# Second layer's rows fetched by quarters, turned by VectorE instead of TensorE, with four output tiles

## The chip, the core and the metric

One core of a Trainium2 chip runs the whole program. The metric is device time in microseconds (us) for one execution; 0.5% of it is about 5 us. The engines are TensorE (PE: matmuls; PEld: its weight loads), VectorE (DVE), ScalarE (ACT), GpSimd (POOL) and SyncE (SP, which here only issues DMAs). Line numbers (L708) are those of the kernel before.

## What is computed

Three steps, each feeding the next (cut to what matters):

```python
x = attention(q, k, v, M_prev, z_prev, beta)        # 4 x 576 tokens, 8 heads of 64 -> 2304 x 512
# layer 1: one expert of 8 for each token
e = argmax(x @ w_gate + modality_bias[modality_id]); x = gate * relu(x @ w1[e]) @ w2[e]
# layer 2: two experts of 8 for each token, chosen with noise
logits = x @ w_gate2 + log1p(exp(x @ w_noise)) * noise
for e in range(8):
    for k in range(2):
        mask = top2[:, k] == e
        out[mask] += top2_w[mask, k, None] * (np.maximum(x[mask] @ w1[e], 0) @ w2[e])
```

Widths are D = 512 for a token and F = 1024 for the hidden layer; everything is float32.

## The kernel before, in words

**Precision.** Each float32 operand is split into a rounded high part and a remainder (`xh`/`xl`, `w1h`/`w1l`, `w2h`/`w2l`, `hh`/`hl`), and each product is three matmuls: high by high, remainder by high, high by remainder (L718 to L720 for `mm1`, L728 to L730 for `mm2`).

**Stages.** Attention runs first; its order on the engines is worked out at build time by a list scheduler (`Tasks`) from costs, priorities and dependencies. The DMAs that fill `out` and part of the DRAM table `xd` with zeros are SP tasks in that plan (L1109 to L1116). Layer 1 then walks over units of 256 tokens of one expert (`full`), or over two half units (`pair`). Each unit gathers its rows, computes them and writes the new tokens `x1` to `xd` (`x1_out`, L882). Beside the matmuls a generator `route2` computes the second layer's routing in small steps; what it finds is added to the table `M2` (L952), which says which slot of which expert holds which token.

**Layer 2** (`layer2`, from L976). Expert 0 is begun on the 256 slots that the last layer 1 unit left (224 used columns). Then `route2` ends, `slot_tables` makes the gather and scatter indices, three 128 row tiles of expert 0 are gathered and the rest of expert 0 runs. After that experts 1 to 7 run in turn, each on 640 slots, that is five tiles of 128. An expert has two stages on TensorE:

- `mm1`: eight blocks `f` of the hidden layer, each as two halves of 304 columns (expert 0: one piece of 384), 12 matmuls each. ACT makes `hh`, DVE makes `hl`, and both split `w2`.
- `mm2`: five tiles (expert 0: three) of 24 matmuls of 512 columns. ACT scales the tile into one of two `os` buffers (L972), and POOL scatters it to `out` with an adding indirect DMA (L973), in which each waits for the landing of the one before.

While `mm2` of expert e runs, expert e+1 is prepared. Five gathers (L701, 128 rows of 520 floats each) were issued on POOL at the start of expert e. A list `todo` is worked off between half tiles. It has eight splits of `w1` (`split_w1`) and five `xsplit`s: four TensorE transposes of 128x128 into PSUM (L708), an ACT copy to `xh` (L709) and a DVE subtraction to `xl` (L710). The transposes stand in TensorE's in-order stream between the matmuls of `mm2`. The weights of expert e+1 are loaded by SP when their buffers are free.

## Time and profile before

| | us |
|---|---|
| runs shown | 986.49, 987.15, 991.69 |
| their median | 987.15 |
| the profiled execution | 984.86 |
| its span on the chip (first to last instruction) | 983.1 |

| engine | busy us | share of the span |
|---|---|---|
| PE (matmul) | 943.0 | 96% |
| DVE | 555.5 | 56% |
| ACT | 488.2 | 50% |
| POOL | 353.2 | 36% |

Attention lasts to about 260 us, layer 1 to about 508, the first 256 slots of layer 2 and its tables to about 540, the experts to about 969; the last scatters and the end of the program follow. A busy share is an average over stages with different limits, so the stages are read one by one. A row of the timeline has start, duration, engine, line, operation, output<-input, and in brackets the idle time before it with what ended that.

### The profile page before, as it was taken

The numbers are of one execution on the slowest core, as the hardware profiler recorded it, in microseconds if no ns is written. First come the engines' busy times: TensorE is split into PE (matmuls) and PEld (weight loads), VectorE is DVE, ScalarE is ACT, GpSimd is POOL, SyncE is SP. The second block draws the span as 40 slices with busy tenths as digits, with TensorE's granted clock in tenths as the row PEclk, the third lists the DMA queues.
The fourth block names the chain that finished last, engine by engine and source line by source line (L and its number), as shares of the span: only waits on it lengthen the run. The fifth ranks groups of instructions, "written<-read, shape, count | busy, mean of one in ns | idle before, by whom it ended". The sixth has DMA issues, their size and how long they took to land. (4 is left out here: it accounts for less than half of the span.)

```text
span 983.1 us, 18583 instructions
## 1 busy us (share of the span) xinstructions
PE 943.0 (96%) x6849; PEld 831.0 (85%) x6849; DVE 555.5 (56%) x1695; ACT 488.2 (50%) x1141; POOL 353.2 (36%) x420
## 2 busy tenths in 40 slices
PE   7999999999989999999997999999999999999994
PEld 5888888888875889888886999898989989898983
DVE  8777777789745577777775244243442424244320
ACT  6887878775433455555552244333342433343320
POOL 5222232244643567777765231121313021231111
PEclk9999999999989899999999999999999999999997
DMA  8345856262567555666655254536446354535112
GB/s 211 100 112 183 270 184 205 93 223 84 167 214 265 162 193 206 216 215 215 205 178 158 66 137 124 127 82 160 105 107 172 97 121 128 138 77 117 23 23 35
DMA packets 83840, 144.98 MB, mean 147 GB/s; under 512 B 14480, under 2 KB 32912, under 8 KB 83728
## 3 DMA queue, kind: packets, MB, share of 16 engines
q1 hardware_dynamic: 73168, 117.10, 36.4%
q0 software_dynamic: 10560, 26.47, 13.6%
q8 instruction: 60, 0.98, 0.4%
q14 instruction: 52, 0.43, 0.1%
HBM read 111.65 MB, written 31.97 MB: 146 GB/s over the span
## 5 line engine op out<-in xcount | busy, mean ns | idle before, releaser
L718 PE MATMUL b<-xh,w1h 128*128 128x304 f32 (+3 forms) x800 | 240.0, 300 | 3.1 <-ACT xh L709 1.3
L719 PE MATMUL b<-xl,w1h 128*128 128x304 f32 (+3 forms) x800 | 238.2, 298 | 3.8 <-DVEq L788 3.5
L720 PE MATMUL b<-xh,w1l 128*128 128x304 f32 (+3 forms) x800 | 237.1, 296 | 0.0
L723 DVE SCALAR_TENSOR_TENSOR hl<-b,hh 128x304 fp32r<-128x304 f32 (+3 forms) x200 | 90.7, 454 | 207.1 <-ACT hh L721 205.4
L728 PE MATMUL b<-w2h,hh 128*128 128x512 f32 x464 | 188.7, 407 | 0.0
L730 PE MATMUL b<-w2h,hl 128*128 128x512 f32 x464 | 182.2, 393 | 0.0
L973 POOL DMA_INDIRECT out_dram<-os,l2s x40 | 62.8, 1571 | 331.5 <-ACT os L972 253.3
L729 PE MATMUL b<-w2l,hh 128*128 128x512 f32 x464 | 181.6, 391 | 0.0
L721 ACT ACTIVATE hh<-b 128x304 fp32r<-128x304 f32 (+3 forms) x200 | 81.8, 409 | 172.7 <-PE b L720 172.6
L718 PEld LDWEIGHTS b<-xh,w1h 128*128 128x128 f32 x800 | 152.7, 191 | 9.3 <-DVE hl L723 4.1
L719 PEld LDWEIGHTS b<-xl,w1h 128*128 128x128 f32 x800 | 152.7, 191 | 4.8 <-DVEq L788 3.7
L720 PEld LDWEIGHTS b<-xh,w1l 128*128 128x128 f32 x800 | 152.9, 191 | 0.0
L730 PEld LDWEIGHTS b<-w2h,hl 128*128 128x128 f32 x464 | 87.5, 189 | 19.5
L729 PEld LDWEIGHTS b<-w2l,hh 128*128 128x128 f32 x464 | 88.0, 190 | 15.5
L728 PEld LDWEIGHTS b<-w2h,hh 128*128 128x128 f32 x464 | 87.7, 189 | 15.4
L151 ACT ACTIVATE p<-sm,l 128x128 f32<-128x128 f32 (+4 forms) x144 | 84.1, 592 | 16.9 <-DVE l L147 16.9
L698 DVE TENSOR_TENSOR w1l<-w1r,w1h 128x512 fp32r<-128x512 f32 x84 | 71.3, 857 | 22.0 <-ACT w1h L697 21.8
L710 DVE TENSOR_TENSOR xl<-b,xh 128x512 fp32r<-128x512 f32 x56 | 38.6, 689 | 73.9 <-ACT xh L709 73.7
L693 ACT CAST w2h<-w2r 128x512 fp32r<-128x512 f32 x128 | 78.5, 613 | 0.0
L709 ACT CAST xh<-b 128x512 fp32r<-128x512 f32 x56 | 32.9, 587 | 87.7 <-PE b L708 87.7
L697 ACT CAST w1h<-w1r 128x512 fp32r<-128x512 f32 x128 | 74.7, 620 | 0.3 <-DMA w1r<-in_w_dram 0.3
L972 ACT ACTIVATE os<-b,l2w 128x512 f32<-128x512 f32 x40 | 27.7, 691 | 94.1 <-PE b L730 47.6
(460 smaller groups left out, 1511.4 us busy)
## 6 DMA issues: line engine op xcount, KB each, us to landing
w1r<-in_w_dram SPq DMA_DIRECT2D x18, 2048.0 KB, 9.6
w2r<-in_w_dram SPq DMA_DIRECT2D x18, 2048.0 KB, 9.2
xd<-gs SPq DMA_DIRECT2D x24, 260.0 KB, 3.7
xd<-x SPq DMA_DIRECT2D x10, 520.0 KB, 10.3
out_dram<-gs SPq DMA_DIRECT2D x19, 256.0 KB, 4.0
k<-in_k_dram SPq DMA_DIRECT2D x16, 256.0 KB, 4.3
q<-in_q_dram SPq DMA_DIRECT2D x16, 256.0 KB, 3.5
v<-in_v_dram SPq DMA_DIRECT2D x16, 256.0 KB, 4.4
```

The source lines that it names most:

```text
L151: s.nc.scalar.activation(s.P[b,i,u][:,lh*n:lh*n+n],s.SM[b,i,u][:,lh*n:lh*n+n],AF.Exp,scale=-1.0,bias=L[:,0,c:c+1],accum_out=L[:,1,c:c+1])
L693: nc.scalar.copy(hi[c],raw[:,c])
L697: nc.scalar.copy(s.w1h[:,:,fs],s.w1r[:,:,fs])
L698: eng.tensor_sub(s.w1l[:,:,fs],s.w1r[:,:,fs],s.w1h[:,:,fs].bitcast(FT))
L718: nc.tensor.matmul(h[:,:n],s.w1h[:,k,fs],s.xh[:,k,cs],start=k==0,stop=False)
L719: nc.tensor.matmul(h[:,:n],s.w1h[:,k,fs],s.xl[:,k,cs],start=False,stop=False)
L720: nc.tensor.matmul(h[:,:n],s.w1l[:,k,fs],s.xh[:,k,cs],start=False,stop=k==KD-1)
L721: def mm1_a(s, h, f, c0, n): s.nc.scalar.activation(s.hh[:,f,c0:c0+n],h[:,:n],AF.Relu)
L723: cs=slice(c0,c0+n); s.nc.vector.scalar_tensor_tensor(s.hl[:,f,cs],h[:,:n],0.0,s.hh[:,f,cs].bitcast(FT),op0=OP.max,op1=OP.subtract)
L728: nc.tensor.matmul(y,s.hh[:,f,cs],s.w2h[f],start=f==0,stop=False)
L729: nc.tensor.matmul(y,s.hh[:,f,cs],s.w2l[f],start=False,stop=False)
L730: nc.tensor.matmul(y,s.hl[:,f,cs],s.w2h[f],start=False,stop=f==KF-1)
```

## The change

**Layout.** `x1_out` writes each pair of tiles twice: to `xd` as before and to a second DRAM table `xq` in which a token is four rows of 128 floats. The zero fill does the same for the slots that need it (24 more DMAs; the groups in the plan become seven instead of five).

**Gathers.** A tile of 128 tokens is fetched by four indirect DMAs of 128 quarter rows (512 bytes each) instead of one of 128 whole rows. DMA i puts quarter g of token 32i+t on partition 32g+t, in columns 128i to 128i+127. The indices `gq4` come from `quarter_tables`: `M2` is copied, four small matmuls with a selection matrix `sel4` (made by `quarter_sel` on POOL) spread it over the partitions, and two DVE operations finish it. Groups of four are spread over the expert: one at its start, two behind `hl` of blocks 3 and 6, two in `mm2` behind `w1l` (expert 0: 2, 4, 6 and one in `mm2`); a one column copy to `pace` on POOL makes each wait.

**Transposes.** `bsplit` turns the tile by one VectorE instruction that transposes blocks of 32x32, into one of two SBUF buffers `xt_`; ACT's copy and DVE's subtraction read that instead of PSUM. Partition p then holds features 4p to 4p+3, so layer 2's `w1` is loaded in that order (`by='(p c)'`). Expert 0's first three gathered tiles still go the old way.

**Output tiles.** `os` has four buffers instead of two; the two new ones lie where `ol2` and part of `yt` lay.

```diff
+        s.xq=s.dram.tile([4*SLOTS,D//4],FT,name='xq')
...
-        ...; s.os=cut(K0,8192,512,'os',2)
+        ...; s.os=cut(K0,8192,512,'os',2)+[T(OL,0,512,'os2'),T(K1,8704,512,'os3')]
...
+    def bsplit(s, g, c0):
+        nc=s.nc; x=s.xt_[s.xn%2]; s.xn+=1
+        nc.vector.transpose(x.rearrange('p j (s t) -> p s j t',s=4),g.rearrange('p (s d j) -> p s j d',s=4,j=KD))
+        nc.scalar.copy(s.xh[:,:,c0:c0+128],x)
+        nc.vector.tensor_sub(s.xl[:,:,c0:c0+128],x,s.xh[:,:,c0:c0+128].bitcast(FT))
...
-        s.nc.sync.dma_start(d[:,c:c+n] if isinstance(c,int) else d[:,bass.ds(c,n)],s.x1[:,:n])
+        ...; dq=s.xq[:].rearrange('(c p q) d -> p c (q d)',p=128,q=4)
+        for d,w in ((d,XW),(dq,D)): s.nc.sync.dma_start(d[:,c:c+n] if isinstance(c,int) else d[:,bass.ds(c,n)],s.x1[:,:n,:w])
...
+    def quarter_sel(s):
+        G=s.nc.gpsimd; f=s.sel4f
+        G.memset(f,0.0)
+        G.affine_select(f.rearrange('p s (g t) -> p s g t',g=4),f.rearrange('p s (g t) -> p s g t',g=4),pattern=[[-32,4],[0,4],[-1,32]],compare_op=OP.not_equal,fill=1.0,base=0,channel_multiplier=1)
+        G.tensor_copy(s.sel4,f)
+        for g in range(4): G.memset(s.qn[32*g:32*g+32],float(g))
+    def quarter_tables(s):
+        ...
+        V.tensor_copy(m,s.M2[:,0])
+        p=s.ps.tile([128,512],FT,name='sm')
+        for i in range(4): nc.tensor.matmul(p[:,i*NC2:(i+1)*NC2],s.sel4[:,i],m,start=True,stop=True)
+        V.tensor_scalar(f,p[:,:4*NC2].rearrange('p (s c) -> p s c',s=4),float(S0),0.0,op0=OP.add,op1=OP.max)
+        V.tensor_scalar(s.gq4,f,4.0,s.qn[:,0:1],op0=OP.mult,op1=OP.add)
+    def quarter_gather(s, c, t, behind=None):
+        if behind is not None: s.nc.gpsimd.tensor_copy(s.pace,behind.bitcast(FT))
+        for i in range(4):
+            s.nc.gpsimd.indirect_dma_start(out=s.gq[t][:,i*128:(i+1)*128],out_offset=None,in_=s.xq[:],in_offset=bass.IndirectOffsetOnAxis(ap=s.gq4[:,i,c+t:c+t+1],axis=0))
...
+            if f==5: s.quarter_sel()
             s.split_w(s.w2r,s.w2h,s.w2l,f,nc.vector if f<3 else nc.gpsimd)
...
             s.l2_out(wk,y,tb,t,out)
+        s.quarter_tables()
         for t in range(NE+2,T2): s.xsplit(ps,ge[t-NE],t*128)
...
-                g=s.l2_gather(wk,tb,(e+1)*TS)
+                s.quarter_gather((e+1)*TS,0)
...
+                at=(2,4,6) if not e else (3,6)
+                if nxt and f in at: s.quarter_gather((e+1)*TS,1+at.index(f),s.hl[:,f,C2-1:C2])
...
-            for t in range(T2): todo.insert(2*t+1,lambda t=t:s.xsplit(ps,g[t],t*128))
+            for t in range(T2): todo.insert(2*t+2 if t<4 else len(todo),lambda t=t:s.bsplit(s.gq[t],t*128))
+            later=[(0,4)] if not e else [(0,3),(2,4)]
...
+                        i=2*(t-ts[0])+q
+                        if later and i==later[0][0]: s.quarter_gather((e+1)*TS,later.pop(0)[1],s.w1l[:,0,(i+1)*128:(i+1)*128+1])
...
+            dma.append(lambda r=r: nc.sync.dma_start(M.xq[4 * (r - N):4 * (r - N) + 512].rearrange('(p q) d -> p (q d)', q=4), zt[:, :D]))
-        M.later = [Q.add(100 * (5 + j // 5), SP, 1000, f, [A.sunk[4 + j // 5]]) for j, f in enumerate(dma)]
+        M.later = [Q.add(100 * (5 + j // 7), SP, 1000, f, [A.sunk[4 + j // 7]]) for j, f in enumerate(dma)]
```

## Rows read from the trace of the kernel before

**Rows 1.** Busy time by stretch: attention, layer 1, layer 2's experts; columns in the first line.
```profile
core 0: us, PE busy (x) PEld busy (x) DVE busy (x) ACT busy (x) POOL busy (x), PEclk, DMA share, GB/s
0.00:260.00 260.00, 249.48 (x2604) 213.14 (x2605) 202.95 (x820) 195.25 (x543) 85.08 (x112) 0.99 0.55 172
322.00:508.00 186.00, 185.12 (x1266) 164.59 (x1266) 142.58 (x433) 105.30 (x224) 130.96 (x173) 0.99 0.60 200
562.00:915.00 353.00, 353.00 (x2068) 319.45 (x2067) 138.27 (x234) 134.18 (x266) 80.06 (x62) 1.00 0.48 119
```

**Rows 2.** Groups of PE instructions by line, 545 to 903 us: the transposes.
```profile
L708 PE MATMUL b<-ident,gs 128*128 128x128 f32 x140 | 20.8, 272 | 0.0
```

**Rows 3.** Timeline of PE in expert 6: one block of transposes.
```profile
888.02 0.39 PE L730 MATMUL b<-w2h,hl 128*128 128x512 f32 x1
888.25 0.60 PE L708 MATMUL b<-ident,gs 128*128 128x128 f32 x4
888.61 0.48 PE L728 MATMUL b<-w2h,hh 128*128 128x512 f32 x1
888.92 0.40 PE L729 MATMUL b<-w2l,hh 128*128 128x512 f32 x1
```

**Rows 4.** Busy time by stretch: mm1 of expert 6, mm2 of experts 6 and 7.
```profile
858.84:885.50 26.66, 26.66 (x193) 26.66 (x192) 12.45 (x23) 11.10 (x24) 8.29 (x7) 1.00 0.35 73
885.50:915.17 29.67, 29.67 (x143) 24.51 (x141) 9.31 (x15) 10.02 (x18) 6.29 (x4) 1.00 0.51 107
941.84:969.06 27.22, 27.22 (x122) 22.35 (x120) 0.67 (x2) 3.18 (x5) 6.20 (x4) 1.00 0.30 37
```

**Rows 5.** Timelines of PE and DVE where the rest of expert 0 begins.
```profile
537.23 1.04 PE L708 MATMUL b<-ident,gs 128*128 128x128 f32 x8
538.49 0.69 DVE L710 TENSOR_TENSOR xl<-b,xh 128x512 fp32r<-128x512 f32 x1 [1.13 <-ACT xh L709]
539.55 0.69 DVE L710 TENSOR_TENSOR xl<-b,xh 128x512 fp32r<-128x512 f32 x1 [0.37 <-ACT xh L709]
539.57 0.45 PE L718 MATMUL b<-xh,w1h 128*128 128x384 f32 x1 [1.30 <-ACT xh L709]
```

**Rows 6.** Busy time by stretch, just behind that: the granted clock is PEclk.
```profile
541.30:544.70 3.40, 3.40 (x12) 3.40 (x12) 0.56 (x1) 0.49 (x1) 2.79 (x3) 0.52 0.95 164
545.00:547.00 2.00, 2.00 (x13) 2.00 (x12) 0.30 (x1) 0.49 (x1) 1.65 (x2) 1.00 0.74 216
```

**Rows 7.** Timelines of POOL, DVE and PE before the tables, and two POOL groups by line.
```profile
524.03 1.28 POOL L694 TENSOR_TENSOR w2l<-w2r,w2h 128x512 fp32r<-128x512 f32 x1 [1.50 <-ACT w2h L693]
524.05 1.29 DVE L941 SCALAR_TENSOR_TENSOR b<-ri,sv 128x4 f32<-128x4 int32 x1
525.26 0.72 POOL L938 CAST wh<-w__8256 128x4 fp32r<-128x4 f32 x1
527.82 0.74 PE L949 MATMUL b<-rrm,ol 128*128 128x256 f32 x4 [0.67 <-DVE rrm L946]
...
L1100 POOL MEMSET gs<- 128x520 f32 x1 | 0.5, 539 | 0.0
L123 POOL TENSOR_SCALAR ph<-q 128x512 f32<-128x512 f32 x4 | 5.9, 1491 | 9.1 <-PE b L175 8.9 <-DVE l L147 0.2
```

**Rows 8.** Gathers: timeline of POOL, landing of layer 2's, and the slowest form.
```profile
541.19 1.02 POOL L701 DMA_INDIRECT gs<-xd,l2g  x1 [0.30 <-issue]
542.51 0.98 POOL L701 DMA_INDIRECT gs<-xd,l2g  x1 [0.30 <-issue]
...
DMA to landing us min/median/max: 3.6/3.9/5.8
...
L701 POOL DMA_INDIRECT gs<-xd,nxi x10: 1250/1388/1499, 381.7 to 488.2; - x10
```

**Rows 9.** One line's instructions on DVE, ns min/median/max, whole span.
```profile
L694 DVE TENSOR_TENSOR w2l<-w2r,w2h x83: 684/693/715, 252.0 to 941.3; 128x512 fp32r<-128x512 f32 x83
```

More of the change, by code (lines that the diff above doesn't have):

```diff
@@ L357, in blocks @@
         K0,K1,X,HL,W2,G,X1,OL=range(8)
-        s.w1r=V(T(K0,0,4096,'w1r'),KD); s.w2r=V(T(K0,4096,4096,'w2r'),KF); s.os=cut(K0,8192,512,'os',2)
+        s.w1r=V(T(K0,0,4096,'w1r'),KD); s.w2r=V(T(K0,4096,4096,'w2r'),KF); s.os=cut(K0,8192,512,'os',2)+[T(OL,0,512,'os2'),T(K1,8704,512,'os3')]
         s.w1h=V(T(K1,0,4096,'w1h',FR),KD); s.w1l=V(T(K1,4096,4096,'w1l',FR),KD); s.yt=V(T(K1,8192,1024,'yt'),KD); s.rr=c.tile([128,4,256],FR,name='rrm')
@@ L365, in blocks @@
         s.wb1=V(T(W2,0,4096,'wb1'),KD); s.wb2=V(T(W2,4096,4096,'wb2'),KF)
+        s.gq=cut(G,0,D,'gq',GB); s.xt_=[V(t,KD) for t in cut(X1,0,D,'xtq',2)]; s.xn=0; s.sel4=V(T(K1,8192,512,'sel4',FR),4); s.sel4f=V(T(K1,8704,512,'sel4f'),4)
         s.x1=V(T(X1,0,2*XW,'x1'),2); s.ol2=V(T(OL,0,512,'ol2',FR),4); s.gs=cut(G,0,XW,'gs',GB); s.gn_=s.on_=0
@@ L686, in tasks, with load_w @@
         Q.add(P+14,POOL,300,lambda:nc.gpsimd.memset(s.rr[:,:,4*NC2:].bitcast(FT),0.0))
-    def load_w(s, raw, w, e, eng=None):
-        src=(w[bass.ds(e,1)] if not isinstance(e,int) else w[e:e+1]).rearrange('o (c p) f -> p (o c) f',p=128)
+    def load_w(s, raw, w, e, eng=None, by='(c p)'):
+        src=(w[bass.ds(e,1)] if not isinstance(e,int) else w[e:e+1]).rearrange('o %s f -> p (o c) f'%by,p=128)
         (eng or s.nc.sync).dma_start(raw,src)
@@ L703, in o, with xsplit @@
     def o(s):
-        s.on_+=1; return s.os[s.on_%2]
-    def xsplit(s, ps, g, c0):
+        s.on_+=1; return s.os[s.on_%len(s.os)]
+    def bsplit(s, g, c0):
[3 more added lines that the diff above has]
+        nc.vector.tensor_sub(s.xl[:,:,c0:c0+128],x,s.xh[:,:,c0:c0+128].bitcast(FT))
+    def xsplit(s, ps, g, c0, fourth=False):
         nc=s.nc
         tp=ps.tile([128,KD,128],FT,name='tp')
-        for k in range(KD): nc.tensor.transpose(tp[:,k],g[:,k*128:(k+1)*128],s.ident)
+        for k in range(KD): nc.tensor.transpose(tp[:,k],g[:,k:D:4] if fourth else g[:,k*128:(k+1)*128],s.ident)
         nc.scalar.copy(s.xh[:,:,c0:c0+128],tp)
@@ L736, in state @@
         nc=s.nc; c=s.c
+        s.qn=c.tile([128,1],FT,name='qn'); s.pace=c.tile([128,1],FT,name='pace')
         s.run=c.tile([128,E],FT,name='run'); nc.gpsimd.memset(s.run,float(DEAD))
@@ L880, in x1_out @@
     def x1_out(s, c, n):
-        d=s.xd[N:].rearrange('(c p) d -> p c d',p=128)
-        s.nc.sync.dma_start(d[:,c:c+n] if isinstance(c,int) else d[:,bass.ds(c,n)],s.x1[:,:n])
+        d=s.xd[N:].rearrange('(c p) d -> p c d',p=128); dq=s.xq[:].rearrange('(c p q) d -> p c (q d)',p=128,q=4)
+        for d,w in ((d,XW),(dq,D)): s.nc.sync.dma_start(d[:,c:c+n] if isinstance(c,int) else d[:,bass.ds(c,n)],s.x1[:,:n,:w])
     def route2(s, wk, ps, u, nt):
@@ L973, in l2_out @@
         nc.gpsimd.indirect_dma_start(out=out,out_offset=bass.IndirectOffsetOnAxis(ap=si[:,c:c+1],axis=0),in_=o,in_offset=None,compute_op=OP.add)
+    def quarter_sel(s):
[5 more added lines that the diff above has]
+    def quarter_tables(s):
+        nc=s.nc; V=nc.vector; m=s.c.tile([128,NC2],FR,name='mq'); f=s.c.tile([128,4,NC2],FT,name='fq'); s.gq4=s.c.tile([128,4,NC2],I32,name='gq4')
+        V.tensor_copy(m,s.M2[:,0])
[7 more added lines that the diff above has]
+            s.nc.gpsimd.indirect_dma_start(out=s.gq[t][:,i*128:(i+1)*128],out_offset=None,in_=s.xq[:],in_offset=bass.IndirectOffsetOnAxis(ap=s.gq4[:,i,c+t:c+t+1],axis=0))
     def l2_gather(s, wk, tb, c, ts=range(T2)):
@@ L983, in layer2 @@
         s.finish(); s.x1_out(s.nf*2+(FC-4),2)
-        s.load_w(s.w1r,w1,E+1)
+        s.load_w(s.w1r,w1,E+1,by='(p c)')
         s.chain=s.route2(wk,ps,NF+NP2,2); s.hold=0
@@ L1013, in layer2 @@
             if nxt:
-                if e: s.load_w(s.w1r,w1,E+e+1)
-                g=s.l2_gather(wk,tb,(e+1)*TS)
+                if e: s.load_w(s.w1r,w1,E+e+1,by='(p c)')
+                s.quarter_gather((e+1)*TS,0)
             for f in range(KF):
@@ L1077, in overflow @@
                 e=nc.values_load(ov[0:1,o:o+1],engines=[ET.SP],min_val=0,max_val=E-1)
-                s.load_w(s.w1r,w1,e+E); s.load_w(s.w2r,w2,e+E)
+                s.load_w(s.w1r,w1,e+E,by='(p c)'); s.load_w(s.w2r,w2,e+E)
                 for ff in range(KF): s.split_w1(ff,nc.vector)
-                for t,g in enumerate(s.l2_gather(wk,tb,o*T2)): s.xsplit(ps,g,t*128)
+                for t,g in enumerate(s.l2_gather(wk,tb,o*T2)): s.xsplit(ps,g,t*128,True)
                 for ff in range(KF):
```

## The prediction

> **What bounds the kernel now.** I read the busy times by stretch first [rows 1]. From 562 to 915 us, where experts 1 to 7 run, PE is busy for 353.00 of 353.00 us at a granted clock of 1.00, while DVE has 138, ACT 134 and POOL 80. Nobody keeps PE waiting there: whatever leaves PE's in-order stream in this stretch shortens the run by its whole length, and work given to DVE, ACT or POOL is free as long as its result comes in time. In attention PE is busy for 249 of 260 us and in layer 1 for 185 of 186, so those stages are bound by PE as well, and the change takes nothing from PE there. Next I read the groups by line for what leaves (140 transposes of L708 between 545 and 903 us [rows 2]), then PE's timeline around one block for its price [rows 3], and last the place where the new tables are made [rows 5 to 7].
>
> **The change part by part.**
>
> *Transposes leave PE.* An `xsplit` is four transposes, so 140 of them are 35 blocks, five in each of seven experts. In [rows 3] a matmul of 512 columns starts 0.23 us after the one before (888.02 to 888.25). From the first transpose to the second matmul behind the block it is 0.67 us (888.25 to 888.92), of which 0.23 is that first matmul's own, so a block costs 0.44 us. 35 x 0.44 = 15.4 us. A second reading bounds it: `mm2` of expert 6 takes 29.67 us with five blocks and of expert 7 without any 27.22 us [rows 4]. The 2.45 us of difference hold 2.2 us of blocks and 0.25 us of matmuls that run slightly slower beside the splits of ACT and DVE; 7 x 2.45 = 17.2 us is the upper end. I take 15.4, since ACT and DVE still do the splits.
>
> *What takes their place.* DVE gets one block transpose of 128x512 per tile. The trace has none; DVE operations of that size take 0.69 us [rows 9]. In `mm2` DVE is busy for 9.31 of 29.67 us [rows 4], so five transposes are hidden up to (27.2 - 9.3) / 5 = 3.6 us each. ACT's copy and DVE's subtraction stay, with the other source. Cost 0.
>
> *Gathers.* Each expert has 20 gathers of 64 KB instead of 5 of 260 KB. On POOL one gather starts 1.3 us after the other (541.19, 542.51) and layer 2's land 3.9 us after issue, 5.8 at most [rows 8]. A group of four then takes 5.3 us, five groups 26 us of an expert of about 54, with five scatters beside them. I follow the latest group for experts 1 to 6, from the start of the expert. Block 6 has its `hl` at 7/8 of 26.66 us [rows 4] and about 1.3 us more, 24.6. Three groups follow, with a scatter and its wait between them (about 1.9): POOL is done at 42.4, the rows are there at 46.3 and split (transpose, copy, subtraction) at 48.3. They are wanted by the second half of the next expert's first block, at 26.66 + 27.22 + 1.67 (26.66 / 16) = 55.5. So 7 us are to spare. Queued on POOL behind the `pace` waits are only further gathers and the scatters; the scatters come up to 4 us later, for which the four `os` buffers are there. Cost 0.
>
> In expert 0 it is tight. Its `mm1` has 96 matmuls of 384 columns (26.66 / 192 x 384 / 304 = 0.175 us each), 16.8 us, and its three tiles 3 x 5.44 = 16.3 us, so the last rows are wanted after 16.8 + 16.3 + 1.7 = 34.8 us. The group behind block 2 can start at about 7.3 us, and four groups in a row end at 28.5; landing (3.9) and split (2.0) give 34.4. I count 0, but see the first rival.
>
> *The tables.* `quarter_tables` stands in PE's stream between the second and third block of transposes at the start of expert 0, and its matmuls wait for a DVE copy that is queued behind the second tile's subtraction. Before, both blocks go as one run at 537.23, that subtraction ends at 539.18, and `mm1` begins at 539.57, when the third tile's ACT copy is done [rows 5]. Now: 539.18, the copy of 48 columns 0.2, four small matmuls 0.5, the third block 0.44, the ACT copy and its hand-overs 0.75, so `mm1` begins at about 541.1, and its second matmul moves with the third subtraction by as much. Everything behind moves too: +1.6 us (1.0 to 2.5).
>
> *The clock there.* [...] I take 0.
>
> *The selection matrix.* `quarter_sel` puts three POOL operations on 512 columns and four short ones ahead of the `w2l` split of block 5. [Rows 7] bound the long ones by 0.54 us (a memset of 520) and 1.49 us (one input, 512 columns); with the short ones 2.0 to 4.9 us. I take 2.6, nearer to the memset, since none of them calculates. POOL has 1.50 us of idle time before its last split, so `wh` (525.26), which `route2` ends on and for which DVE and then PE's L949 wait (0.67), comes about 1.1 us later. The first gathers come later by as much, but they wait today behind a weight load that does not move, so part of it is absorbed. +0.8 us (0 to 2.5). DVE can suffer beside POOL: an operation on four columns that starts with a POOL split lasts 1.29 us, as long as the split [rows 7]. [...] The rows speak against it for gathers: two-input splits of 128x512 last 0.715 us at most, though some run beside gathers [rows 9].
>
> *DMAs.* The second `x1_out` DMA (0.5 MB) stands on SP ahead of a weight load in each layer 1 unit, and the zero fill has 24 more in attention. The mean DMA share is 0.60 and 0.55 [rows 1], and PE is at 185 of 186 us, so loads come early enough now. The plan of attention sees more SP tasks ahead of its loads, which are issued several chunks early. +0.3 us (-1.5 to +2). The other order of `w1` moves the same 2 MB, in longer runs: 0. The two more `os` buffers shorten no wait of PE; at the end each scatter waits for the one before, not for a buffer: 0.
>
> *Sum.* -15.4 + 1.6 + 0 + 0.8 + 0.3 = -12.7 us. The profiled execution took 984.86 us (span 983.1), so the same execution would take 972.2. It lies 2.3 us below the median of the runs, 987.15; taken off that, 974.5 us.
>
> **The rivals.**
>
> 1. *Expert 0's last group is late.* It has 0.4 us to spare. In layer 1 the gathers by `nxi` take 1.39 us on POOL instead of 0.95 to 1.02 [rows 8]. If quarter gathers are of that kind, the pitch is 1.7, the 16 gathers in a row end 6 us later, and PE stands still for 5.5 us and gets the lower clock again (1.6): 974.5 + 7 = 981.5 us. For it: no row shows a gather of 512 byte rows. Against: the same form of index, and smaller pieces to land.
>
> 2. *POOL becomes the bound, and the kernel slower than before.* With pitch p, experts 1 to 6 need 24.6 + 12p + 7.8 us and have 55.5, so it decides from p = 1.93; expert 0 loses 16 (p - 1.3) - 0.4. At p = 2.2 that is 6 x 12 x 0.27 + 14 = 33 us: about 1008 us. It undoes the gain from p = 2.0 up. Against: the slowest gather, 1.50 us with 0.30 between, makes 1.8 [rows 8]. [...]
>
> 3. *DVE becomes the bound, no change.* At 4.1 us per transpose DVE needs all that PE gave back in `mm2`, and the time is about 986 us. Its read steps over four floats, which no row shows; but six times the price of any DVE operation of this size would be needed.
>
> **How the numbers follow.** About 0.5% (5 us) is what a measurement of this kernel can tell from no change. The forecast has a chance of 0.73. With all its terms at their good ends it gives 984.86 - 17.2 + 1.0 - 1.6 - 1.5, a gain of 19.3, so 967.9; at their bad ends a gain of 15.4 - 2.5 - 1.6 - 2.5 - 2 = 6.8, so 980.4. Rival 1 has 0.15, rival 2 0.05, rival 3 0.04; 0.03 is for a plan of attention that comes out otherwise, to either side. The range goes from 968 to 982, to take in the forecast and rival 1. Faster by over 0.5% (below 982.2) is the forecast and most of rival 1: 0.86. Within 0.5% is rival 3 and the rest of rival 1: 0.08. Slower: 0.06.
>
> **What would show it.** Right: no L708 between the matmuls of `mm2` from expert 0 on; `mm2` of experts 1 to 6 at 27.2 to 27.5 us and an expert at 54.1 instead of 56.3; PE's busy share there still 100% at clock 1.00; `mm1` of expert 0 begins 1 to 2.5 us later behind L949, with one stretch of low clock. Wrong: a wait of PE for `xh` or `xl` at the second half of an expert's first block (rival 1 in expert 1 only, rival 2 in all); POOL's pitch above 1.9 us; DVE busy through `mm2`; the starts of layer 1 or layer 2 moved by over 2 us, which would mean that DMAs or the plan matter.

## The result, and the profile after

The changed kernel took 995.59 us (median of 7 runs, 992.60 to 999.13), the kernel before in the same set of runs 987.15 us (985.97 to 991.69): a ratio of 1.0073, 95% interval 1.0048 to 1.0098. I had forecast 974.5 us. The number can't be understood without one more: the same kernel, unaltered, was measured three more times, each beside its own runs of the kernel before, and came out at 0.9886, 1.0114 and 0.9890. In two of the six sets of runs of this study something disturbs this kernel far more than the one before, and the first measurement is one of the two. The experiments' recorded texts call these two sets slow, the other four fast.

The profile after, by stages. Each is the difference of two starts on PE's timeline; "first" and "second product" are `mm1` and `mm2`, and the last column is the same program in an undisturbed set (run `again`, below).

| Stage | before | after | again |
|---|---|---|---|
| up to layer 2's first product | 508.06 | 512.61 | 509.55 |
| from there to expert 0 | 31.51 | 33.45 | 34.03 |
| expert 0, first product | 18.89 | 18.52 | 19.40 |
| expert 0, second product | 18.71 | 24.42 | 16.36 |
| expert 1, first product | 26.67 | 26.67 | 26.97 |
| experts 2 to 6, first products, sum | 133.34 | 146.75 | 133.37 |
| experts 1 to 6, second products, sum | 177.99 | 163.34 | 163.36 |
| from expert 7 to the end | 67.93 | 68.14 | 68.26 |
| span | 983.1 | 993.9 | 971.3 |

The trace of before is of an execution of 984.86 us, under all seven of the first set (985.97 and more). The gain is there in all its size: 14.65 us in the second products of experts 1 to 6. What ate it are stalls in two other places: 8.06 us in expert 0's second product and 13.38 us in the first products of experts 2 to 6, against `again`. Busy time by stretch of the changed kernel (first line: columns): expert 0's second product, expert 2's first product, expert 6's second product, expert 7's first product. The third answers to the 29.67 us of [rows 4].

```profile
core 0: us, PE busy (x) PEld busy (x) DVE busy (x) ACT busy (x) POOL busy (x), PEclk, DMA share, GB/s
564.58:589.00 24.42, 19.29 (x74) 15.06 (x73) 13.93 (x19) 8.90 (x16) 13.20 (x14) 0.86 0.27 61
642.89:673.52 30.63, 28.48 (x193) 28.23 (x192) 12.59 (x23) 11.00 (x24) 15.84 (x16) 0.94 0.29 47
898.54:925.76 27.22, 27.22 (x122) 22.53 (x121) 14.33 (x20) 10.44 (x18) 17.50 (x16) 1.00 0.55 134
925.76:952.43 26.67, 26.67 (x193) 26.66 (x192) 12.45 (x23) 11.10 (x24) 3.13 (x2) 1.00 0.17 22
```

The same four stages of the same program in `again`:

```profile
562.98:579.34 16.36, 16.36 (x74) 13.51 (x73) 12.73 (x18) 8.30 (x15) 12.82 (x13) 1.00 0.19 47
633.54:660.21 26.67, 26.67 (x194) 26.67 (x192) 12.47 (x23) 11.10 (x24) 13.80 (x15) 1.00 0.31 50
875.81:903.04 27.23, 27.23 (x122) 22.53 (x121) 14.18 (x20) 10.34 (x18) 17.53 (x16) 1.00 0.53 132
903.04:929.71 26.67, 26.67 (x193) 26.66 (x192) 12.45 (x23) 11.10 (x24) 3.13 (x2) 1.00 0.18 25
```

In the first measurement PE is idle for 5 us of expert 0's second product and 2 us of expert 2's first, and the granted clock falls behind each gap (to 0.50, from 577 to 583 us and from 669 to 672; 0.86 and 0.94 over the stage). What PE waits for can be seen in both places. Timeline of ACT and then of POOL in expert 2 of the changed kernel (start, duration, engine, line, operation; in brackets the idle time before it and what ended it, where `issue` says that the profile shows nothing that it waited for):

```profile
663.29 0.42 ACT L729 ACTIVATE hh<-b 128x304 fp32r<-128x304 f32 x1 [0.92 <-PE b L728]
667.55 0.42 ACT L729 ACTIVATE hh<-b 128x304 fp32r<-128x304 f32 x1 [3.83 <-PE b L728]
667.87 0.61 ACT L695 CAST w2h<-w2r 128x512 fp32r<-128x512 f32 x1
...
664.22 0.95 POOL L1001 DMA_INDIRECT gq<-xq,gq  x1 [0.30 <-issue]
665.47 0.94 POOL L1001 DMA_INDIRECT gq<-xq,gq  x1 [0.30 <-issue]
```

And PE at the same time:

```profile
665.95 0.30 PE L727 MATMUL b<-xl,w1h 128*128 128x304 f32 x1
666.09 0.30 PE L728 MATMUL b<-xh,w1l 128*128 128x304 f32 x1
668.53 0.41 PE L726 MATMUL b<-xh,w1h 128*128 128x304 f32 x1 [2.15 <-DVE hl L731]
668.92 0.44 PE L728 MATMUL b<-xh,w1l 128*128 128x304 f32 x1
```

PE waits for a PSUM bank that DVE has to read, DVE waits for ACT, and ACT starts `hh` at 667.55 although the product it needs was finished at about 664.7 (its last matmul, of 0.30 us, started at 664.44), and in the program this `hh` waits for PE alone. ACT goes on 1.1 us after the eighth gather of an unbroken row has left POOL (665.47 + 0.94). Experts 3 to 6 show the same, each near the end of such a row. In expert 1, where POOL pauses for 1.7 us between the first two groups, there is no stall.

In expert 0 it is PE itself that stands still, in the middle of a block that waits for nothing (timeline of PE, changed kernel). Sixteen gathers run on POOL from 556.6 to 577.0 us, with less than 0.7 us between any two:

```profile
572.33 0.39 PE L737 MATMUL b<-w2l,hh 128*128 128x512 f32 x1
574.29 0.40 PE L738 MATMUL b<-w2h,hl 128*128 128x512 f32 x1 [1.58 <-issue]
576.39 0.39 PE L736 MATMUL b<-w2h,hh 128*128 128x512 f32 x1 [1.70 <-issue]
577.13 0.59 PE L737 MATMUL b<-w2l,hh 128*128 128x512 f32 x1 [0.35 <-issue]
579.22 0.58 PE L738 MATMUL b<-w2h,hl 128*128 128x512 f32 x1 [1.50 <-issue]
```

The trace of this execution is itself incomplete: the list of DMA issues has no landing time for any of GpSimd's DMAs (first two lines), where that of `again`, and that of the kernel before [rows 8], have them (last two; kind, count, us from issue to landing). Of the 20 traces of this study four lack them, and these are the four of the two disturbed sets: this one, `again2`, `tables` and `before_os4`.

```profile
gq<-xq,gq POOLq DMA_INDIRECT x140
out_dram<-os,l2s POOLq DMA_INDIRECT x40
```

```profile
gq<-xq,gq POOLq DMA_INDIRECT x140, 2.7
out_dram<-os,l2s POOLq DMA_INDIRECT x40, 4.9
```

### The profile page after: what moved, and what is told of

The parts are those of the page before. It is cut to its first block, busy times and chain, and to the rows that moved or that the text cites. A ratio compares the mean times of both kernels' runs of the same rounds, so it can differ in the third digit from the quotient of the medians.

```text
span 993.9 us, 18456 instructions
## 1 busy us (share of the span) xinstructions
PE 934.7 (94%) x6713; PEld 821.1 (83%) x6713; DVE 591.6 (60%) x1733; ACT 490.3 (49%) x1141; POOL 472.5 (48%) x560
## 3 DMA queue, kind: packets, MB, share of 16 engines
q0 software_dynamic: 12240, 26.33, 13.4%
## 5 line engine op out<-in xcount | busy, mean ns | idle before, releaser
L726 PE MATMUL b<-xh,w1h 128*128 128x304 f32 (+3 forms) x800 | 241.2, 301 | 12.7 <-DVE hl L731 10.7
L736 PE MATMUL b<-w2h,hh 128*128 128x512 f32 x464 | 186.1, 401 | 1.7 <-issue 1.7
L1001 POOL DMA_INDIRECT gq<-xq,gq x140 | 145.8, 1042 | 42.4 <-issue 40.0
L151 ACT ACTIVATE p<-sm,l 128x128 f32<-128x128 f32 (+4 forms) x144 | 84.0, 591 | 17.2 <-DVE l L147 17.2
L696 POOL TENSOR_TENSOR w2l<-w2r,w2h 128x512 fp32r<-128x512 f32 x45 | 59.0, 1313 | 34.4 <-ACT w2h L695 26.4
L147 DVE CUSTOM_DVE_ANT_0 sm<-b,mask 128x128 f32<-128x128 f32 (+4 forms) x144 | 63.0, 479 | 12.4 <-PE b L139 8.5
```

Source lines behind the costliest of these rows:

```text
L151: s.nc.scalar.activation(s.P[b,i,u][:,lh*n:lh*n+n],s.SM[b,i,u][:,lh*n:lh*n+n],AF.Exp,scale=-1.0,bias=L[:,0,c:c+1],accum_out=L[:,1,c:c+1])
L726: nc.tensor.matmul(h[:,:n],s.w1h[:,k,fs],s.xh[:,k,cs],start=k==0,stop=False)
L736: nc.tensor.matmul(y,s.hh[:,f,cs],s.w2h[f],start=f==0,stop=False)
L1001: s.nc.gpsimd.indirect_dma_start(out=s.gq[t][:,i*128:(i+1)*128],out_offset=None,in_=s.xq[:],in_offset=bass.IndirectOffsetOnAxis(ap=s.gq4[: ...
```

## The experiments

My first theory was that a long unbroken row of gathers holds up ACT and PE. Its rival was that the cause is the load of w1: as ACT and DVE are no longer paced by PE's transposes, the splits of w1 end 16.5 us into the second product instead of 21, SP starts the next 2 MB then, and they meet the last group of gathers and the scatters (in expert 1 DVE waited 7.7 us for a gather there, and 9.7 us passed from one scatter to the next).

### The changed kernel again

No edit, three times, `again`, `again2` and `again3`:

> The changed kernel, unaltered, on the chip and beside the runs of the kernel before that the others of this set are compared with. In its first trace ACT and PE stood still in places where no edit of the experiments so far changes anything (5.7 us in the second matrix product of expert 0, some 4 us ahead of layer 2), and these stalls were not in the traces of the two edited kernels. If they belong to the kernel, they are there again: ratio to before 1.005 to 1.010, expert 0's second product 22 to 25 us, first products of experts 2 to 6 28 to 31 us. If they belong to that execution, expert 0's second product takes 16.4 us, and what is left of the loss in experts 2 to 6 is what the early load costs: 1 to 2 us an expert, as in the kernel with spaced groups, ratio 0.990 to 0.997.

> The changed kernel unaltered once more, beside its own runs of the kernel before. Twice measured so far, it came out on both sides: 995.6 against 987.2 us the first time, with stalls of ACT and PE that no wait of the program explains and with the landing records of half the gathers missing from the trace, and 971.8 against 981.9 us the second time, without them. If the stalls were a disturbance of the first measurement: ratio 0.987 to 0.991, first matrix products of experts 1 to 6 at 26.7 to 27.0 us, expert 0's second product 16.4 us. If the kernel itself falls into either case: a ratio near 1.007 again, or runs of both kinds.

> The changed kernel unaltered, a third time, as the measure of the other three of this set. Expected by the kind of the set alone: ratio 0.987 to 0.991 where the kernel before takes 982 to 985 us, 1.005 to 1.012 where it takes 987 us or more. A ratio between these, or one that goes with the other time of before, would say that the two kinds of sets are not what divides the results.

Measured: 971.80 us against 981.92 (0.9886, interval 0.9861 to 0.9910); 999.06 against 988.09 (1.0114, 1.0083 to 1.0144); 972.08 against 983.25 (0.9890, 0.9873 to 0.9906). `again` and `again3` have expert 0's second product at 16.36 us and the first products of experts 2 to 6 at 26.66 to 26.70. `again2` has 25.33 and 29.25, 29.13, 28.85, 31.24 and 30.51, expert 1 at 26.67, and no landing times of GpSimd's DMAs: the first trace once more. So the kernel does fall into two cases, with nothing between, and the kernel before moves with them by 5 us (982 to 984, and 987 to 988). The number of the chip doesn't tell them apart: the same number had one set of each kind.

### The load and the distance of the groups

`held` and `held2` put the last split of w1 behind the fifth tile, so that SP's load comes at 21 us again:

```
+            if e:
+                w7=todo.pop(-2); wait=lambda:None
+                todo[-1:]=[wait,todo[-1],wait,w7]
```

> The changed kernel with the last split of w1 put two slots later (behind the split of the fifth tile), so that SP starts the next load of w1 about 21 us into the second matrix product, as before the change, and not at 16.5 us. Theory 2 (the 2 MB load that now falls on the last group of gathers and on the adding scatters is what makes the rest late): the scatters of experts 1 to 6 keep to 5.6 us from one to the next, the first group of the next expert ends 14 us into its first matrix product and not 18 us, the stall of 1.7 to 4 us an expert goes, 980 to 986. Theory 1 (a row of eight gathers) expects the same gain where the first two groups come apart by 1 us or more, and no gain where they still touch. A third view, that the load is hidden anyway, expects 993 to 998.

> The changed kernel with the load of w1 held back, once more. In its first set (the kernel before at 984 us) it took 0.9885 of that; the unaltered kernel, in a set of the same kind, 0.9886, so that holding the load back was worth nothing there. In a slow set (the kernel before at 987 to 989 us): if the meeting of the load with the last gathers and scatters counts, 0.990 to 1.000; if the rows of gathers count, 1.003 to 1.012, with 28 to 31 us for the first products of experts 2 to 6, as in the unaltered kernel.

`spaced` puts a pause between the first groups:

```
-                at=(2,4,6) if not e else (3,6)
+                at=(2,4,6) if not e else (5,7)
```

> The changed kernel with one edit: in experts 1 to 6 the second and third group of gathers go behind hl 5 and hl 7 in place of hl 3 and hl 6, so that on POOL a pause of some 2 us stands between the late first group and the second. Theory 1 (it is the unbroken row of eight gathers, 0.3 us apart, that holds up ACT and with it PE): the stall in the first matrix product of experts 2 to 6 goes, that product takes 26.7 us in each where the changed kernel took 30.6, 29.5, 28.4, 28.9 and 29.4, and the kernel gains about 13 us: 980 to 985. Theory 2 (the stall is a consequence of the late weight load and scatters, or of reading hl on POOL, whatever the spacing): the stall stays or moves with the second group, 992 to 997.

`spread` puts one ahead of every group, and holds the load back as well:

```
+            if e:
+                x4=todo.pop(); w7=todo.pop(); wait=lambda:None
+                todo+=[wait,wait,wait,w7,wait,x4]
-            later=[(0,4)] if not e else [(0,3),(2,4)]
+            later=[(0,4)] if not e else [(2,3),(4,4)]
```

> The changed kernel with a pause of 1.5 us or more ahead of every group of experts 1 to 6: second and third group behind hl 5 and hl 7, fourth and fifth behind the fourth and sixth split of w1, the split of the fifth tile last, and the load of w1 held back to about 21 us into the second product. If it is the rows of eight and more gathers that cost in the slow sets, this kernel loses no more than 1 us an expert there and is 0.990 to 0.998 of the kernel before, where the changed kernel unaltered is 1.007 to 1.011; the stall of expert 0, whose groups are not touched, stays (+6 to 8 us). If the number of gathers and not their spacing counts, 1.005 or more. In a fast set: 0.986 to 0.991, as the changed kernel.

`unpaced` and `unpaced2` go the other way, with twenty gathers in one row:

```
-                at=(2,4,6) if not e else (3,6)
-                if nxt and f in at: s.quarter_gather((e+1)*TS,1+at.index(f),s.hl[:,f,C2-1:C2])
+                at=(1,2,3,4)
+                if nxt and f in at: s.quarter_gather((e+1)*TS,1+at.index(f))
-            later=[(0,4)] if not e else [(0,3),(2,4)]
+            later=[]
```

> The changed kernel with no pacing: all five groups of an expert are issued one behind the other in the first matrix product, twenty gathers in a row, and none in the second; the load of w1 stays early (16.5 us into the second product). If what costs is that the load and the last group meet, this removes the meeting without touching the load: the first matrix products of experts 1 to 6 take 26.7 us, and the ratio to before is 0.985 to 0.990, as with the load held back. If long rows of gathers cost PE or ACT something, or if scatters that queue behind them hold up the output tiles, it is 0.995 or more.

> The changed kernel with all twenty gathers of an expert in one row, a second time. In a fast set it was as fast as the unaltered kernel (0.9890 and 0.9886), so that pacing and spreading bring nothing there: the same again. In a slow set, if long rows of gathers are what costs, it is the slowest of the four, over 1.02, with more than 30 us in each first product of experts 1 to 6; if the load of w1 is what costs, which meets no gather here, 0.990 to 1.000.

All of these met undisturbed sets. `held` 0.9885 (0.9862 to 0.9908) and 0.9906 (0.9885 to 0.9926): the same as the unaltered kernel, so there the meeting of load, gathers and scatters costs PE nothing by itself. That refutes the rival for these sets; for a disturbed one it was not seen. `unpaced` 0.9890 (0.9866 to 0.9914) and 0.9881 (0.9865 to 0.9898): pacing and spreading bring nothing either. `spaced` is slower, 0.9937 (0.9912 to 0.9961; 977.10 us beside 972.03 of `held` in the same set), and `spread` slower than the kernel before, 1.0211 (1.0180 to 1.0242). Their pauses push the last group behind its time, and in `spaced` the load makes it later still. Timelines of POOL and DVE in `spaced`, the last gather of expert 1 and the transpose that needs it:

```profile
625.01 0.95 POOL L1001 DMA_INDIRECT gq<-xq,gq  x1 [0.30 <-issue]
...
633.22 1.08 DVE L710 STREAM_TRANSPOSE xtq<-gq 128x512 f32<-128x512 f32 x1 [8.74 <-DMA gq<-xq,gq]
```

7.3 us from POOL to DVE, while the 2 MB of w1 are on their way. This gather leaves POOL 21.0 us after the start of the second product, 17.1 in `again`, and PE waits 1.1 us for it: the unaltered kernel has 2 to 3 us in hand there, and they are what hides the load. With the load held back that reserve is 6.6 to 7.7 us in experts 1 to 6 (`held` and `held2`). Waits of PE and of DVE in `spread`, experts 2 to 7 (waiting line, releaser: us in total, times, longest):

```profile
PE b L726 <- ACT xh L711: 16.1, 5, 3.6
...
DVE xtq L710 <- DMA gq<-xq,gq: 78.3, 16, 9.1
```

This is the wait for `xh` at the second half of an expert's first block, the one that the prediction names as the sign of a late group. It comes five times, up to 3.6 us, and with the lower clock behind it (granted 0.95 over expert 2's first product, 0.90 over expert 3's) the first products of experts 2 to 6 take 31.7 to 33.7 us. In expert 2 the last gather leaves POOL 25.6 us after the start of the second product, 17.4 in `again`.

What pacing does buy shows on POOL. In `unpaced` each expert's first gather comes later than the last one's: 11.9 us after the start of expert 2 (632.40), 22.5 us after that of expert 6 (847.97). In `again` it is 12.7 and 13.3 (633.54 and 849.11). Timeline of POOL, two gathers of `unpaced`, then two of `again`:

```profile
644.33 1.02 POOL L1001 DMA_INDIRECT gq<-xq,gq  x1 [0.30 <-issue]
870.47 1.01 POOL L1001 DMA_INDIRECT gq<-xq,gq  x1 [0.30 <-DVE hl L731]
```

```profile
646.20 1.02 POOL L1001 DMA_INDIRECT gq<-xq,gq  x1 [0.30 <-issue]
862.42 1.12 POOL L1001 DMA_INDIRECT gq<-xq,gq  x1 [0.30 <-issue]
```

Twenty gathers in a row take 27.6 us (644.33 to 671.92) and the five scatters behind them 27.3 (672.22 to 699.52): three start 5.6 to 6.0 us after the one before, which has to land first, and one 8.3. From one expert's first gather to the next one's it is 54.9 to 57.6 us of POOL, in an expert of 53.9. Pacing lets gathers run while a scatter lands; in one row they don't. Seven experts are too few for the drift to cost much: 1.35 us in expert 6, where ACT waits 5.8 us for an output buffer. In `unpaced2` the drift is smaller (17.1 us in expert 6) and costs nothing.

### Rows of gathers alone

`bursts`, three times: the kernel before with gathers that nothing reads.

```
+    def burst(s, w1, tb, c, a, b, behind=None):
+        if behind is not None: s.nc.gpsimd.tensor_copy(s.pace,behind.bitcast(FT))
+        for i in range(a,b):
+            s.nc.gpsimd.indirect_dma_start(out=s.dq[i],out_offset=None,in_=w1.rearrange('e c (q f) -> (e c q) f',f=128),in_offset=bass.IndirectOffsetOnAxis(ap=tb[0][:,c+i%T2:c+i%T2+1],axis=0))
...
+                for a,b,at in {1:[(0,4,4)],2:[(0,8,4)],3:[(0,12,4)],4:[(0,16,4)],5:[(0,4,4),(4,8,6)],6:[(0,8,0)]}.get(e,[]):
+                    if f==at: s.burst(w1,tb,e*TS,a,b,s.hl[:,f,C2-1:C2])
```

> The kernel before with added gathers of 128 pieces of 512 bytes into tiles that nothing reads, in the first matrix product, behind hl 4 on POOL: 4 in expert 1, 8 in a row in expert 2, 12 in expert 3, 16 in expert 4, 4 and 4 with a pause in expert 5, and 8 from the start of expert 6, right behind the five gathers of whole rows. Theory 1 (a long unbroken row of gathers alone holds up ACT and PE): 26.67 us for the first matrix product of experts 1 and 5, over 28 us for experts 2 to 4, the most in expert 4. Theory 2 (waits between the gathers and what reads them, or the load): 26.67 us in all of them, but for scatters that come late.

> The kernel before with added gathers that nothing reads, once more: 4 in expert 1, 8 in a row in expert 2, 12 in expert 3, 16 in expert 4, 4 and 4 with a pause in expert 5, 8 right behind the five of whole rows in expert 6. The first time it ran in a set in which the kernel before took 984 us, and no first matrix product grew (26.67 to 26.79 us). In sets in which the kernel before takes 987 to 989 us the changed kernel loses 2 to 4 us an expert near the eighth gather of a row. If rows of gathers alone do that in such a set: 26.7 to 27.8 us in expert 1, 28 to 32 us in experts 2 to 4 and 6, growing with the row, and less in expert 5. If the losses need the readers, the scatters or the load beside the gathers: 26.7 to 27.8 us in all. In a set with the kernel before at 982 to 985 us: 26.7 us in all, as before.

> The kernel before with rows of 4, 8, 12, 16, 4 and 4, and 8 added gathers that nothing reads, a third time. Both times so far it met a set of the fast kind and cost nothing. In a slow set: if rows of gathers alone hold up ACT and PE, the first products of experts 2, 3 and 4 grow by 1.5 us and more, expert 4's the most, and experts 1 and 5 by under 1 us; if readers or scatters are needed, none by over 1.1 us. In a fast set: 26.7 us in all but expert 5, whose last groups came late twice (26.8 and 28.1 us).

Measured: 983.65 us (a single run) against 984.25, 984.21 against 982.97 (1.0007, 0.9995 to 1.0020), 983.33 against 983.25 (1.0011, 1.0000 to 1.0023). All three sets were undisturbed. Busy time by stretch, the first product of expert 2 with eight added gathers and of expert 4 with sixteen (first `bursts`):

```profile
632.41:659.08 26.67, 26.67 (x194) 26.67 (x192) 12.50 (x23) 11.10 (x24) 14.68 (x15) 1.00 0.38 87
745.08:771.75 26.67, 26.67 (x194) 26.67 (x193) 12.51 (x23) 11.10 (x24) 14.74 (x15) 1.00 0.40 86
```

A row of sixteen gathers, 1.25 us apart, takes nothing from PE or ACT. One product is longer, expert 5's in `bursts2` at 28.12 us, where ACT waits 7.6 us for an output buffer. In this form the first theory is refuted: a row of gathers alone is no sufficient cause. In a disturbed set the probe was not seen, so what rows do there rests on the place of the stalls (expert 1 against experts 2 to 6), on `tables` below, where a row of twenty gathers met a disturbed set and lost the most, and on `before_os4`, which had rows of five.

### Four output buffers

`held_os2` is `held` with two buffers, `before_os4` the kernel before with four:

```
-s.os=cut(K0,8192,512,'os',2)+[T(OL,0,512,'os2'),T(K1,8704,512,'os3')]
+s.os=cut(K0,8192,512,'os',2)
```

> The kernel with the load held back, with two buffers for output tiles as before the change in place of four. I priced the buffers at nothing. If so: the same time as with four, within 2 us, ratio 0.986 to 0.991. If the spread groups delay the scatters so far that ACT waits for a free buffer: the second matrix products of experts 1 to 6 grow above 27.22 us by 1 us or more each, or the first ones above 26.67, ratio 0.992 or more.

> The kernel before with four buffers for output tiles and nothing else of the change. With two buffers the changed kernel lost 2.2 to 3.4 us of PE at the start of each expert, ACT waiting for a scatter. The kernel before has 6 us more between its scatters and its first matrix product, and PE does not wait there: expected the same time as before, ratio 0.998 to 1.002. If the buffers help this kernel too, the start of experts 1 to 7 shows it, ratio below 0.997.

With two buffers the changed kernel takes 1001.87 us, 1.0209 (1.0172 to 1.0247), 30 us more than `again` in the same set. The kernel before with four takes 988.93 against 988.09, 1.0010 (0.9990 to 1.0030): nothing. Timeline of ACT in `held_os2`, expert 2, and PE's wait in that stage:

```profile
637.66 0.69 ACT L981 ACTIVATE os<-b,l2w 128x512 f32<-128x512 f32 x1 [8.49 <-DMA out_dram<-os,l2s]
638.25 0.41 ACT L729 ACTIVATE hh<-b 128x304 fp32r<-128x304 f32 x1
...
PE b L726 <- DVE hl L731: 2.3, 1, 2.3
```

Eight gathers stand on POOL ahead of an expert's first scatter, and the scatters land one after the other. So ACT waits 8.5 us for a buffer, 4 us into the next expert, and that expert's first `hh` stands behind it on ACT. PE stops for 2.3 us and goes on at the lower clock (granted 0.94 over the stage): 30.78 us for a first product of 26.67.

`before_os4` met the second disturbed set, and its trace shows the disturbance in a kernel without any quarter gathers. Timeline of ACT and then of POOL in its expert 2, where five gathers of whole rows stand in a row, and its list of DMA issues:

```profile
646.52 0.42 ACT L721 ACTIVATE hh<-b 128x304 fp32r<-128x304 f32 x1 [1.26 <-issue]
649.00 0.42 ACT L721 ACTIVATE hh<-b 128x304 fp32r<-128x304 f32 x1 [1.54 <-PE b L720]
...
647.64 1.35 POOL L701 DMA_INDIRECT gs<-xd,l2g  x1 [0.30 <-issue]
...
gs<-xd,l2g POOLq DMA_INDIRECT x38
```

The `hh` at 649.00 comes 0.8 us later than its place in the pattern (1.54 us idle where the others of its kind have 0.72), at the end of the fifth gather. The same happens in each of experts 1 to 6, and their first products take 27.05 to 27.91 us instead of 26.67, 3.9 us together. That is most of the 5 us by which the kernel before moves with the set, since with two buffers it took as long there (988.09). So the disturbance needs neither quarter gathers nor rows of eight, and here expert 1 is not free of it.

### The preparation, and the table

`prep` is the kernel before with the copy `xq`, its fills, `quarter_sel` and `quarter_tables`, and layer 2 as it was:

```
-                s.quarter_gather((e+1)*TS,0)
+                g=s.l2_gather(wk,tb,(e+1)*TS)
...
-            for t in range(T2): todo.insert(2*t+2 if t<4 else len(todo),lambda t=t:s.bsplit(s.gq[t],t*128))
+            for t in range(T2): todo.insert(2*t+1,lambda t=t:s.xsplit(s.ps,g[t],t*128))
...
```

> The kernel before with the preparation alone: the second copy of the rows to memory, its fills, the selector on POOL and the table of quarter rows; layer 2 gathers whole rows and transposes on TensorE as before, and the tables are used by nothing. If the 4.6 us by which layer 2 starts later in the changed kernel, and the 1.9 us before expert 0, come from these, this kernel takes 991 to 995. If they come from the gathers and their stalls alone, 986 to 989.

Measured: 989.00 us against 984.25, 1.0052 (1.0034 to 1.0071). The preparation costs 4.75 us. About 2 of these lie at the table: from the second product of layer 2's first two tiles to expert 0 it is 18.74 us (526.62 to 545.36), 16.68 in the kernel before. Timeline of PE there in `prep`, which answers to [rows 5]:

```profile
541.47 0.60 PE L716 MATMUL b<-ident,gs 128*128 128x128 f32 x4
543.56 0.62 PE L995 MATMUL b<-mq,sel 128*128 128x48 f32 x4 [1.50 <-DVE mq L993]
544.03 0.66 PE L716 MATMUL b<-ident,gs 128*128 128x128 f32 x4
545.36 0.44 PE L726 MATMUL b<-xh,w1h 128*128 128x384 f32 x1 [0.67 <-ACT xh L717]
```

The rest comes before layer 2, and single traces scatter more than it is: layer 2 begins at 506.3 to 508.6 us in the four undisturbed traces without the preparation, and at 507.8 to 513.0 in the twelve with it, 2.6 us later on average.

`best` puts the whole table behind the third transposes and issues expert 0's groups unpaced, with the load held back as in `held`:

```
-        s.quarter_tables()
         for t in range(NE+2,T2): s.xsplit(ps,ge[t-NE],t*128)
+        s.quarter_tables()
...
-                at=(2,4,6) if not e else (3,6)
+                at=(1,2,3,4) if not e else (3,6)
...
```

`tables` and `tables2`, with the load as in the change, copy the table's input ahead and put its matmuls behind the first block of expert 0:

```
+        s.mq=s.c.tile([128,NC2],FR,name='mq'); V.tensor_copy(s.mq,s.M2[:,0])
...
+                if not e and f==0: s.quarter_tables(); s.quarter_gather(TS,0)
+                at=(1,2,3,4) if not e else (3,6)
...
```

> The kernel with the load held back, with two further edits around expert 0: the table of quarter rows is made behind the transposes of the third tile, where PE doesn't wait for it (the wait cost 1.9 us), and the groups of expert 0 are issued without pacing, all in its first matrix product. Expected: expert 0 begins at about 539.6 us where it began at 541.4 us, expert 1's first product takes 26.7 us, in all 2 to 3 us less than with the load held back alone, ratio 0.984 to 0.988. If the wait for the tables only moves to the first gathers and from there to expert 1, the same as before these edits.

> The changed kernel with the four matrix products of the table of quarter rows put behind the first one of expert 0, their input copied ahead of the transposes, and the groups of expert 0 unpaced behind them. The edit that only put the whole table behind the third transposes left expert 0 at 18.6 us after the start of the second product before it, as with the table ahead of them (18.7 to 19.2), where the kernel before takes 16.7. If PE waited there for the copy and the table alone, this one takes 16.7 again and the kernel gains 2 us against the changed kernel beside it; if the later first group is missed in expert 1, its first product grows beyond 27 us by what was gained.

> The kernel with the table of quarter rows behind the first product of expert 0 and that expert's groups unpaced. In a set of the slow kind it took 1.0226, the row of twenty gathers in expert 0 costing 13 us there. In a fast set: expert 0 starts 16.7 to 17.3 us after the second product before it and not 18.7 to 19.2, and with expert 1 at 27 us the kernel is 2 us faster than the unaltered one beside it, ratio 0.985 to 0.989; if the last group now comes too late, expert 1's first product is over 27.5 us and the gain is gone. In a slow set: 1.015 to 1.025 again.

`best` 0.9907 (0.9882 to 0.9931), no gain: PE now waits 2.19 us for the copy behind the third transposes, and expert 0 starts 18.59 us after the second product as before. `tables` fell into the disturbed set: 1.0226 (1.0199 to 1.0253), with expert 0's second product at 29.79 us behind its row of twenty gathers and expert 1's first at 32.22. In an undisturbed set, `tables2`: 970.18 us against 983.25, 0.9864 (0.9844 to 0.9884), beside 972.08 of the unaltered kernel. Expert 0 starts after 17.24 us and its first product takes 17.77 instead of 19.71. Timeline of PE in `tables2`:

```profile
542.10 0.44 PE L726 MATMUL b<-xh,w1h 128*128 128x384 f32 x1 [1.30 <-ACT xh L717]
...
544.69 0.33 PE L728 MATMUL b<-xh,w1l 128*128 128x384 f32 x1
544.87 0.52 PE L994 MATMUL b<-mq,sel 128*128 128x48 f32 x4
545.23 0.42 PE L726 MATMUL b<-xh,w1h 128*128 128x384 f32 x1
```

The table's matmuls stand there without a wait. In an undisturbed set this is the fastest version of all, 1.4% faster than the kernel before. It is 1.9 us faster than the unaltered kernel beside it (each of its four runs is below each of the other's, though the intervals of the two ratios overlap). In a disturbed set it was the slowest (1010.10 us).

## Why the prediction was right and wrong

The forecast missed the measured time by 21 us and its sign. The step that failed is the premise of its first paragraph, that work given to DVE, ACT or POOL is free as long as its result comes in time, and with it the 0 for the gathers. In that set of runs ACT and PE stood still for 8.1 us in expert 0 and 13.4 us in experts 2 to 6 (table: 24.42 - 16.36, 146.75 - 133.37), without waiting for POOL's results, during POOL's rows of gathers and up to 2 us behind them. Two of the four undisturbed sets have the unaltered kernel and show what the other steps were worth: 10.1 and 11.2 us gained, where the sum has 12.7. Step by step, `again` against the kernel before:

- *Transposes leave PE, 15.4 us, at most 17.2.* The upper end came: 14.63 us in experts 1 to 6 (2.44 each) and 2.35 in expert 0, 17.0 us. The 0.25 us per second product that I put down to the splits of ACT and DVE went with the blocks, though the splits stayed.
- *DVE's block transposes, free.* Right: 1.07 us each, 1.6 times the 0.69 us that I compared them with and far below the 3.6 allowed. Rival 3 is refuted.
- *Gathers, free.* Right in these sets but for 0.3 us, with the pitch as taken (0.94 to 0.97 us for most, 1.49 at most, and 0.30 between). The median landing is 2.7 us where I took 3.9, but the last gather of experts 1 to 5 takes 7.4 to 8.0 us, as it meets a load that I had left at its old place: 1.9 to 2.7 us to spare there, not 7 (expert 6, which no load of `w1` follows, has 7.0). Expert 1 waits 0.3 us, so rival 1's margin of 0.4 came out at -0.3. That it came so near is luck: POOL was done with expert 0's groups 33.1 us after its start and not 28.5, as the first paced group started at 11.4 and not 7.3, and the rows were wanted at 37.4 and not 34.8, as my 16.8 us for its first product leaves out the stretch of low clock (19.4, granted 0.86 over it). Rival 2 names the right engine for a reason that I had not counted: not the pitch but the scatters, each of which lets the next one start only 5.5 us or more later. In one row with the gathers they take POOL beyond the 53.9 us of an expert (`unpaced`), and I counted one scatter of 1.9 us among the gathers.
- *Output buffers, 0.* Wrong as a price. I wrote that the scatters come later and that four buffers are there for it, and then that they shorten no wait of PE. Without them the changed kernel, its load held back, is 30 us slower. The number 0 holds for the kernel before alone.
- *The table, +1.6 (1.0 to 2.5).* Right: 1.9 us from the second tile's transposes to expert 0 (539.35 to 543.58, 4.23; before 2.34).
- *The clock there, 0 (-1.6 to +1.6).* The 1.6 here and in rival 1 is 3.40 - 12/13 x 2.00 = 1.55 us, worked out from [rows 6]; no run shows it as what a longer wait adds or takes away. In its place came +0.5: expert 0's first product 19.40 us (granted clock 0.86 over it) instead of 18.89 (0.91). In `tables2`, with the wait gone, it is 17.77. Single traces can't give this term: of the five of layer 2 as it was and without the table, three take 17.3 us there (granted clock 1.00 in `bursts`) and two 18.9 (0.91 in the one that I read), so the 1.55 us, which I took for the kernel's own cost, had come by chance.
- *The selection matrix +0.8, DMAs +0.3.* Up to expert 0 the rest is 2.1 us in `again` (1.5 before layer 2, 0.6 inside it); `prep` gives 2.75 us (4.75 less 2.0 for the table). About 1 to 1.7 us too small. In the measured set layer 2 started 4.6 us later, beyond the 2 us that the prediction had named as a sign of being wrong; the undisturbed traces give 2.6 on average.
- *The range.* Its good end is written from 984.86 but reckoned from 987.15; from 984.86 it would be 965.6.

So the sum was 12.7, and with measured terms it is 17.0 - 1.9 - 0.5 - 2.1 - 0.3 = 12.2 us for this execution, whose spans differ by 11.8. The rest of this belongs to "from expert 7 to the end", 0.3.

What causes the stalls of the measured set stays open. Shown: they come and go with the set of runs and not with the kernel, the two traces of the unaltered kernel agree in their places, and the early load, rows of gathers without readers and the lack of pauses cost nothing, or next to nothing, in the other sets. Argued only: that rows of gathers bring them on and that longer rows lose more, since five gathers of whole rows cost the kernel before 0.4 to 1.2 us an expert, rows of eight 1.7 to 4.6 us in the two traces, and the rows of sixteen and twenty most; expert 1, whose first row is of four, is free of it in both traces. One more reading goes with the missing landing times: that the recording itself took the time, which is a guess of mine. Counted in the kept traces, 1488 of the 6848 landing records of DMAs are missing from the first one, and 373 of 4624 from that of `before_os4`, which lost less. But by place the two signs do not go together: in the first trace the second products of experts 1 to 6 lack as many as the first ones and lost no time. No run here was made without recording, so this reading is not shown.

## What to carry to other kernels

A chain of adding scatters on GpSimd costs the landing of each (5.6 us here), not its issue (1.6): count that time before you call GpSimd idle, and give the engine that fills the scatters' source enough buffers to run past it. When an engine is relieved, look at what its own pace had been holding back, here the splits, the next weight load and the last gathers, and check each deadline; pauses put between gathers for safety, with the last ones pushed behind their time, turned a gain of 1.1% into a loss of 2.1%. And measure a change in more than one set of runs, against its own runs of before, ahead of explaining a difference of 1%: a trace that lacks records is a warning.

## What the runs showed of the hardware

- One program took 972 us in two sets and 996 to 999 us in two others, with nothing between; the kernel before moved by 5 us, of which 3.9 show in the first products of experts 1 to 6 (`before_os4`).
- A gather of 128 pieces of 512 bytes costs POOL 0.94 to 0.97 us as a rule (1.49 at most) and 0.30 between, and lands after 2.7 us (8.0 at most, where it meets the load of `w1`); one of 128 rows of 2 KB lands after 3.9 [rows 8]. Four of 64 KB were worth more than one of 260 KB in the undisturbed sets: 4 x 1.25 us of GpSimd a tile cost next to nothing (0.3 us of PE's waiting, in expert 1 of `again`), and the layout they bring saved 0.49 us of PE a tile.
- DVE's block transpose of 128x512, reading with a step of four floats, takes 1.07 to 1.09 us, and the subtraction with both inputs in SBUF 0.69 us (0.77 at most) with POOL's gathers beside it: no contention from issuing DMAs is seen.
